# The head of a DiT block: one LayerNorm tile earlier, its transposes ahead of the K product, a PSUM bank for the first scale group, and a K pair split around scale sums

## The chip, the cores and the metric

One core of a Trainium2 chip runs the whole block. The metric is the device time of a run in microseconds. Lower is better.

## The reference, cut to what matters

```python
def reference(x, c, wqkv, wo, w_mod, w_fc1, w_fc2):       # x (2, 256, 1152), bf16
    mod = (_silu(c) @ w_mod).reshape(B, 6, 1, D)
    shift_a, scale_a, gate_a, shift_m, scale_m, gate_m = [mod[:, i] for i in range(6)]
    h = _layernorm(x, axis=-1) * (1 + scale_a) + shift_a  # <- the part that changes
    qkv = (h @ wqkv).reshape(B, N, 3, H, Dh)
    ...                                                   # attention, residual, LN2, MLP
    return x + gate_m * m
```

The kernel treats the 512 tokens as four tiles of 128 (tiles 0 and 1 are batch 0, tiles 2 and 3 batch 1) and the 1152 features as nine k-tiles. It normalises a tile (`xn`), transposes it on TensorE, multiplies it by `1 + scale_a` (`hk`), and starts the K product with the first four k-tiles, for which only the first group of the scales is needed. The scales come from 2-column matmuls (the "scale sums") on weights that arrive in three loads for each of two groups.

## The kernel before

All instructions are recorded as units with their reads and writes; a static scheduler orders them, with TensorE in program order and VectorE (DVE) and ScalarE (ACT) in a given order at the start. What the change touches, with cuts marked:

```python
# waits of the last store
if ins is last_out:
    for o in outs[:-4]:
        eng_handle.wait_ge(dma_sems[o.dma_sem], o.dma_val)
for (k, v) in waits[ins.gidx]:                      # its data: the VectorE result
    ...

# statistics: tiles 1 and 2 on VectorE, tiles 0 and 3 on ScalarE; the power is on GpSimd
pool(650, lambda e: e.tensor_tensor(out=rstd_t, in0=var, in1=NHALF, op=ALU.pow), ...)

XB = [(4, 5, 3), (6, 5, 7)]                         # PSUM banks of the transposes, per batch
...
def mod_kt(W, kt, col0, name, fs=(0, 9)):           # scale sums of one k-tile of the weights
    S.unit("pe", (fs[1] - fs[0]) * 27.0, name)
    for f in range(*fs):
        mm(ps32(7, col0 + f * 2, 2), W[:, kt, f * 128:(f + 1) * 128], ST[:, kt:18:9], False, kt == KT - 1, ...)
...
def sca(k0, k1):                                    # first group: 4 matmuls per k-tile
    for kt in range(k0, k1):
        mod_kt(WSC, kt, 0, "sca_%d" % kt, (0, KC))
...
xn_T(1); warm(1, "c"); sca(0, 3)                    # warm = filler matmuls for the clock
xn_T(0); warm(1, "d"); sca(3, 6)
warm(1, "e"); sca(6, 9)
hk(0, 0); sc1a(0, KC); hk(1, 0)
...
xn_T(3, 0, 8)
k_first(0)                                          # K product, batch 0, k-tile 0
k_first(1)
xn_T(3, 8, 9)
xn_T(2)                                             # nine transposes inside the K product
...
for kt in range(KT):                                # second group: 5 matmuls per k-tile
    mod_kt(WSC, kt, 0, "scb_%d" % kt, (KC, KT))
hk(KC, 0)
...
k_pair(range(KC), 2, 1)                             # 8 matmuls that cover the scaling of k-tile 4
```

## Time and profile before

| | kernel before |
|---|---|
| median of the first 3 runs | 244.39 us (244.12 to 244.48) |
| span of the profiled run | 243.0 us |
| TensorE busy | 238.2 us, 98% |
| first K matmul starts | 11.80 us |
| k-tile 4 of the K product starts | 20.16 us |
| last VectorE operation ends | 241.32 us |
| last store is issued | 241.43 us |

TensorE is the path from the first K matmul to the last product. So the table is read as three stretches: the head up to 11.80, the stretch to k-tile 4, in which the change still moves instructions, and the rest, which it leaves alone apart from the order of the waits at the last store. The lines behind this table are in the prediction. L688 and L691 are the helpers for matmuls and transposes; with one line for many tiles, the shapes and the times tell which is meant. The starts of single matmuls and the landings of loads are from the records behind the views. In the lines, each of which has a start and a length in us, PE is TensorE's matmuls, PEld its weight loads (which overlap them), POOL is GpSimd, SPq the queue that issues loads and stores, and brackets hold the idle time before an instruction and what ended it.

### The profile page before, as it was taken

The page shows a single profiled execution, that of the slowest core. Times are in us where ns is not written, and L with a number is a line of the kernel's source. Part 1 is how long each engine was busy: PE and PEld are TensorE (multiplying, and loading weights), DVE is VectorE, ACT ScalarE, POOL GpSimd, SP SyncE. Part 2 cuts the span into 40 slices and gives each one's busy share as a digit, 9 for nine tenths or more (in the row PEclk, how much of TensorE's full clock was granted, in tenths as well). Part 3 has the DMA queues.
Part 4 walks back from the last instruction along what each step waited for, and adds up shares of the span by engine and source line. Part 5 has one row for each costly group of instructions (what it writes and reads, how often), then busy time and mean ns, then how long its engine had stood idle before and what let it go on. Part 6 is the DMA issues. An engine that isn't in the chain of part 4 may idle for free.

```text
span 243.0 us, 4065 instructions
## 1 busy us (share of the span) xinstructions
PE 238.2 (98%) x1753; PEld 148.0 (61%) x1763; DVE 120.4 (50%) x217; ACT 67.2 (28%) x136; POOL 21.5 (9%) x39
## 2 busy tenths in 40 slices
PE   7999999999999999999999999999999999999996
PEld 2698854556667666898444444444656656666575
DVE  3724379596997899789999600000022222111112
ACT  4730350345424206983233322222000000000000
POOL 1500000000021186400000000020000000000000
DMA  6999999999995999979953498011000000000000
GB/s 237 334 381 392 392 391 391 398 414 405 389 350 170 350 386 393 392 266 392 323 162 82 166 308 323 0 32 68 0 16 19 16 16 19 16 16 19 18 28 21
DMA packets 30140, 51.59 MB, mean 212 GB/s; under 512 B 1703, under 2 KB 15787, under 8 KB 30123
## 3 DMA queue, kind: packets, MB, share of 16 engines
q1 hardware_dynamic: 29680, 50.14, 57.7%
q0 software_dynamic: 416, 1.19, 1.6%
q8 instruction: 14, 0.23, 0.4%
q14 instruction: 3, 0.02, 0.0%
q10 hardware_dynamic: 27, 0.00, 0.0%
HBM read 50.14 MB, written 1.19 MB: 211 GB/s over the span
## 4 chain that ended last, share of the span: by engine, by line
PE 94%; DMA 3%; SPq 1%; issue 0%; DVE 0%
PE psum L688 93%; DMA arena<-in_w_mod_dram 3%; PE psum L691 1%; SPq L669 1%; DVE arena L805 0%; DVE arena L1268 0%; DVE arena L1269 0%
## 5 line engine op out<-in xcount | busy, mean ns | idle before, releaser
L688 PE MATMUL psum<-arena 128*128 128x384 bf16 (+12 forms) x1664 | 234.8, 307 | 2.4 <-POOL arena L711 1.5
L688 PEld LDWEIGHTS psum<-arena 128*128 128x128 bf16 (+3 forms) x1674 | 142.7, 97 | 90.6 <-issue 4.5
L1063 DVE SCALAR_TENSOR_TENSOR arena<-arena 128x1152 f32<-128x1152 bf16 x32 | 44.7, 1414 | 0.6
L1268 DVE TENSOR_TENSOR arena<-psum,arena 128x384 f32<-128x384 f32 (+3 forms) x14 | 7.0, 501 | 68.0 <-PE psum L688 68.0
L1177 ACT ACTIVATE arena<-psum 128x512 bf16<-128x512 f32 (+1 forms) x44 | 22.4, 520 | 42.7 <-PE psum L688 42.7
L683 ACT ACTIVATE arena<-psum 128x512 bf16<-128x512 f32 (+6 forms) x37 | 19.6, 550 | 38.6 <-PE psum L688 37.0
L685 DVE CAST arena<-psum 128x512 bf16<-128x512 f32 (+3 forms) x13 | 8.2, 641 | 11.4 <-PE psum L688 11.3
L669 POOL DMA_DIRECT2D dit_scratch<-arena x3 | 1.8, 617 | 115.6 <-DVE arena L685 58.8
L1145 POOL TENSOR_TENSOR arena<-arena 128x384 f32<-128x384 f32 x12 | 10.9, 914 | 11.4 <-DVE arena L1144 9.8
L1090 DVE CAST arena<-psum 72x32 bf16<-72x32 f32 x1 | 0.2, 187 | 21.3 <-PE psum L688 21.3
L739 DVE BATCH_NORM_STATS2 arena<-arena 128x6 f32<-128x384 f32 (+1 forms) x18 | 9.5, 548 | 0.1
L1150 ACT ACTIVATE arena<-arena 128x1152 bf16<-128x1152 f32 x4 | 5.3, 1344 | 11.1 <-DVE arena L1149 11.1
L1144 DVE TENSOR_TENSOR arena<-psum,arena 128x384 f32<-128x384 f32 x12 | 6.5, 552 | 1.5 <-PE psum L688 0.9
L1269 DVE TENSOR_TENSOR arena<-arena 128x384 bf16<-128x384 f32 (+3 forms) x14 | 7.0, 501 | 0.5
L691 PE MATMUL psum<-arena 128*128 128x128 bf16 (+1 forms) x89 | 7.1, 219 | 0.0
L691 PEld LDWEIGHTS psum<-arena 128*128 128x128 bf16 (+1 forms) x89 | 5.8, 98 | 2.0 <-DMA arena<-in_c_dram 0.8
L1167 ACT ACTIVATE arena<-psum,arena 128x128 bf16<-128x128 bf16 x16 | 6.0, 456 | 1.7 <-PE psum L691 1.1
L1164 DVE TENSOR_SCALAR arena<-psum,arena 128x128 bf16<-128x128 bf16 x20 | 5.4, 336 | 1.9 <-PE psum L691 1.9
L1070 DVE TENSOR_REDUCE arena<-arena 128x36 f32<-128x1152 f32 x4 | 5.4, 1346 | 0.0
L1067 DVE STREAM_TRANSPOSE arena<-arena 128x1152 f32<-128x1152 f32 x4 | 5.4, 1363 | 0.0
L993 ACT ACTIVATE arena<-psum,arena 128x256 bf16<-128x256 f32 x8 | 3.7, 473 | 1.3 <-PE psum L688 0.9
L947 ACT ACTIVATE arena<-arena 128x256 bf16<-128x256 bf16 x6 | 2.6, 498 | 3.9 <-DVE arena L941 3.9
(48 smaller groups left out, 45.8 us busy)
## 6 DMA issues: line engine op xcount, KB each, us to landing
arena<-in_w_fc_dram SPq DMA_DIRECT2D x9, 1152.0 KB, 7.5
arena<-in_w_fc_dram SPq DMA_DIRECT2D x4, 2592.0 KB, 17.4
arena<-in_wqkv_dram SPq DMA_DIRECT2D x18, 288.0 KB, 10.3
arena<-in_w_mod_dram SPq DMA_DIRECT2D x3, 1728.0 KB, 20.4
arena<-in_w_mod_dram SPq DMA_DIRECT2D x3, 864.0 KB, 13.3
arena<-in_w_mod_dram SPq DMA_DIRECT2D x9, 288.0 KB, 10.8
arena<-in_wqkv_dram SPq DMA_DIRECT2D x1, 2592.0 KB, 16.7
arena<-in_wo_dram SPq DMA_DIRECT2D x1, 2592.0 KB, 24.4
```

Source lines behind the costliest of these rows:

```text
L683: act(c_act(n), lambda e: e.activation(out=dst, in_=src, func=ACTF.Copy), [src], [dst], name)
L685: dve(c_dve_psum16(n) if psum16 else c_dve_psum32(n), lambda e: e.tensor_copy(dst, src), [src], [dst], name)
L688: S.instr(lambda e: e.matmul(o, lhsT=l, rhs=r, start=st, stop=sp, **kw), reads=[l, r], writes=[o])
L691: S.instr(lambda e: e.transpose(o, i_, idn), reads=[i_, idn], writes=[o])
L739: dve(550, lambda e, s=s, o=o: e.bn_stats(out=o, in_=s), [s], [o], "bn_%s_%d" % (tag, ci))
L1063: dve(1270, lambda e, w=w, s=s, acc=acc: e.scalar_tensor_tensor(out=acc, in0=w, scalar=s, in1=acc, op0=ALU.mult, op1=ALU.add), [w, s, acc] ...
L1144: dve(550, lambda e, o=o, ga=ga, x1c=x1c: e.tensor_tensor(out=x1c, in0=o, in1=ga, op=ALU.mult), [o, ga], [x1c], "wo_t1_%d_%d" % (t, ci))
L1145: S.op("pool", 930, lambda e, xs=xs, x1c=x1c: e.tensor_tensor(out=x1c, in0=x1c, in1=xs, op=ALU.add), reads=[x1c, xs], writes=[x1c], name=" ...
L1167: act(440, lambda e, o=o, dst=dst, s1=s1, s2=s2: e.activation(out=dst, in_=o, func=ACTF.Identity, scale=s1, bias=s2), [o, s1, s2], [dst], ...
L1177: act(c_act(ntok), lambda e: e.activation(out=dst, in_=o, func=ACTF.Gelu_apprx_tanh), [o], [dst], "gelu_%d_%d" % (f, tok0))
L1268: dve(c_dve_psum32(w), lambda e, o=o, gm=gm, t1=t1: e.tensor_tensor(out=t1, in0=o, in1=gm, op=ALU.mult), [o, gm], [t1], "fc2_t1_%d_%d" % ( ...
L1269: dve(c_dve_32(w), lambda e, t1=t1, x1c=x1c, ost=ost: e.tensor_tensor(out=ost, in0=t1, in1=x1c, op=ALU.add), [t1, x1c], [ost], "fc2_out_%d ...
```

## The change

Its intent: tile 2 takes its statistics early so that tiles 2 and 3 are both transposed before K starts, out of the dense stretch; the first scale group gets bank 1 and its sums are closed first, so that the first `hk` waits for three matmuls in place of twelve; half a K pair moves between the second group's sums, as cover for their last load; the last store waits for its data last. Cut to its core (the orders of VectorE and of the fillers follow suit):

```diff
-                    if ins is last_out: ...wait for the older stores
                     for (k, v) in waits[ins.gidx]: ...
+                    if ins is last_out: ...wait for the older stores
-        XB = [(4, 5, 3), (6, 5, 7)]
+        XB = [(4, 5, 3), (6, 2, 7)]
+        def mod_f0(kt):
+            mm(ps32(1, 0, 2), WSC[:, kt, 0:P], ST[:, kt:18:9], False, kt == KT - 1, ...)
         def sca(k0, k1):
             for kt in range(k0, k1):
-                mod_kt(WSC, kt, 0, "sca_%d" % kt, (0, KC))
+                mod_f0(kt)
+            for kt in range(k0, k1):
+                mod_kt(WSC, kt, 0, "sca_%d" % kt, (1, KC))
         ...
         xn_T(1)
-        warm(1, "c")
         sca(0, 3)
-        xn_T(0)
         warm(1, "d")
         sca(3, 6)
-        warm(1, "e")
+        warm(1, "f", "aggr_ln1_2")
+        xn_T(0)
+        warm(1, "e", "rstd_ln1_2")
+        xn_T(2, 0, 8)
         sca(6, 9)
         ...
         k_first(0)
+        xn_T(3, 8, 9)
+        xn_T(2, 8, 9)
         k_first(1)
-        xn_T(3, 8, 9)
-        xn_T(2)
         ...
         for kt in range(KT):
+            if kt == 6:
+                k12(0)                       # 4 of the pair's 8 matmuls
             mod_kt(WSC, kt, 0, "scb_%d" % kt, (KC, KT))
         ...
-        k_pair(range(KC), 2, 1)
+        k12(1)                               # the other 4
         ...
-        S.order_after(by["rstd_ln1_2"], by["rstd_ln1_3"])
+        S.order_after(by["rstd_ln1_3"], by["rstd_ln1_2"])
```

More of the change, by code (lines that the diff above doesn't have):

```diff
@@ L468, in run_engine @@
                 for ins in u.instrs:
-                    if ins is last_out:
-                        for o in outs[:-4]:
-                            eng_handle.wait_ge(dma_sems[o.dma_sem], o.dma_val)
                     for (k, v) in waits[ins.gidx]:
@@ L476, in run_engine @@
                             eng_handle.wait_ge(sems[k[1]], v)
+                    if ins is last_out:
+                        for o in outs[:-4]:
+                            eng_handle.wait_ge(dma_sems[o.dma_sem], o.dma_val)
                     bi = ins.fn(eng_handle)
@@ L783, in warm @@
                 S.unit("pe", 300.0, "warm_%s_%d" % (tag, i))
-                mm(ps32(2), IDENT, Q4B, True, True)
+                mm(ps32(0), IDENT, Q4B, True, True)
                 if behind:
@@ L791, in mod_kt, with sc1a @@
                 mm(ps32(7, col0 + f * 2, 2), W[:, kt, f * 128:(f + 1) * 128], ST[:, kt:18:9], False, kt == KT - 1, skip_group_check=True)
-        def sc1a(ka, kb):
-            m, o = ps32(7, 2 * ka, 2 * (kb - ka)), SC1A[:, 2 * ka:2 * kb]
+        def sc1a(ka, kb, bank=7):
+            m, o = ps32(bank, 2 * ka, 2 * (kb - ka)), SC1A[:, 2 * ka:2 * kb]
             dve(180, lambda e: e.tensor_copy(o, m), [m], [o], "sc1a_%d" % ka)
@@ L799, in hk @@
             dst = HK[:, kt, b * 256:(b + 1) * 256]
-            s1 = ps32(7, 2 * kt, 1) if kt in (0, KC) and b == 0 else SC1A[:, kt * 2 + b:kt * 2 + b + 1]
+            s1 = ps32(1 if kt == 0 else 7, 2 * kt, 1) if kt in (0, KC) and b == 0 else SC1A[:, kt * 2 + b:kt * 2 + b + 1]
             src = xslot(b, kt) if kt < KC else HX[:, kt, b * 256:(b + 1) * 256]
@@ L812, in k_mm @@
                    kt == KT - 1, skip_group_check=True)
-        KB = [(0, 1, 2, 3), (4, 5, 6)]
+        KB = [(0, 1, 5, 3), (4, 2, 6)]
         ev_rr = [0]
@@ L831, in k_pair @@
                         "k_ev%d_%d" % (b, i))
+        def mod_f0(kt):
+            S.unit("pe", 27.0, "sca0_%d" % kt)
+            mm(ps32(1, 0, 2), WSC[:, kt, 0:P], ST[:, kt:18:9], False, kt == KT - 1, skip_group_check=True)
         def sca(k0, k1):
             for kt in range(k0, k1):
-                mod_kt(WSC, kt, 0, "sca_%d" % kt, (0, KC))
+                mod_f0(kt)
+            for kt in range(k0, k1):
+                mod_kt(WSC, kt, 0, "sca_%d" % kt, (1, KC))
         def sc_ones(ka, kb):
@@ L839, in sc_ones @@
             mm(ps32(7, 2 * ka, 2 * (kb - ka)), IDENT, ONES[:, 2 * ka:2 * kb], True, True)
-        sc_ones(0, KC)
+        S.unit("pe", 30.0, "ones_f0")
+        mm(ps32(1, 0, 2), IDENT, ONES[:, 0:2], True, True)
+        sc_ones(1, KC)
         warm(7, "b")
@@ L845, in build_kernel @@
         xn_T(1)
-        warm(1, "c")
         sca(0, 3)
-        xn_T(0)
         warm(1, "d")
         sca(3, 6)
-        warm(1, "e")
+        warm(1, "f", "aggr_ln1_2")
+        xn_T(0)
+        warm(1, "e", "rstd_ln1_2")
+        xn_T(2, 0, 8)
         sca(6, 9)
         hk(0, 0)
-        sc1a(0, KC)
+        sc1a(0, 1, 1)
+        sc1a(1, KC)
         hk(1, 0)
@@ L886, in build_kernel, with k12 @@
         k17(0, 0, KC)
+        def k12(half):
+            S.unit("pe", KC * c_mm(256), "k1_2%d" % half)
+            k_mm(range(KC), 4 + half, 1, KB[1][2], half)
         for kt in range(KT):
+            if kt == 6:
+                k12(0)
             mod_kt(WSC, kt, 0, "scb_%d" % kt, (KC, KT))
@@ L956, in build_kernel @@
             "dve": ["zq4b", "c_half", "c_silu", "bn_ln1_1_0", "bn_ln1_1_1", "bn_ln1_1_2", "aggr_ln1_1", "veps_ln1_1", "bn_ln1_2_0",
-                    "xn_1", "bn_ln1_2_1", "xn_0", "bn_ln1_2_2", "aggr_ln1_2", "var_ln1_3", "veps_ln1_2", "xn_3", "hk_0_0", "sc1a_0", "hk_1_0",
-                    "xn_2", "hk_0_1", "hk_1_1", "hk_2_1", "hk_3_1", "hk_%d_0" % KC, "sc1a_4", "hk_%d_1" % KC] + ["hk_%d_%d" % (kt, b) for kt in range(KC + 1, KT) for b in range(2)],
+                    "bn_ln1_2_1", "xn_1", "bn_ln1_2_2", "aggr_ln1_2", "veps_ln1_2", "xn_0", "var_ln1_3", "xn_2", "xn_3", "hk_0_0", "sc1a_0", "sc1a_1", "hk_1_0",
+                    "hk_0_1", "hk_1_1", "hk_2_1", "hk_3_1", "hk_%d_0" % KC, "sc1a_4", "hk_%d_1" % KC] + ["hk_%d_%d" % (kt, b) for kt in range(KC + 1, KT) for b in range(2)],
             "act": ["ld_c", "c_tanh", "sum_ln1_0", "sq_ln1_0", "sum_ln1_3", "sq_ln1_3", "xnT_cp0_4", "xnT_cp0_8", "hk_2_0", "hk_3_0",
```

## The prediction

> **What bounds the kernel now.** I read the page's busy shares first, then the chain that ended last in order of time, then the timeline of the first 32 us, and last the semaphore and DMA-landing records behind the trace.
>
> ```profile
> PE 238.2 (98%) x1753; PEld 148.0 (61%) x1763; DVE 120.4 (50%) x217; ACT 67.2 (28%) x136; POOL 21.5 (9%) x39
> ```
>
> TensorE is busy for 98% of the span. Time is only won where it stands still on the chain, where useless work on it disappears, or in the tail after its last matmul. The chain, with start, length and what:
>
> ```profile
> 2.87 7.88 DMA arena<-in_w_mod_dram
> 10.75 0.05 issue
> 10.79 0.47 PE psum L688 x12
> 11.26 0.14 PE psum L691 x2
> 11.39 0.36 DVE arena L805
> 11.75 0.05 issue
> 11.80 1.92 PE psum L688 x16
> 13.72 0.56 PE psum L691 x10
> 14.28 19.14 PE psum L688 x234
> ...
> 240.84 0.24 DVE arena L1268
> 241.07 0.02 issue
> 241.10 0.23 DVE arena L1269
> ```
>
> L688 is a matmul, L691 a transpose, L805 the product of a transposed LN1 tile and the attention scale (hk). The third scale load lands at 10.75, twelve 2-column scale matmuls follow, DVE makes hk of k-tile 0 (11.39 to 11.75), and the K product starts at 11.80. From there TensorE runs almost without a hole; ten transposes of 56 ns (tile 2, and a rest of tile 3) stand inside the K product. So two figures count: when K starts (call it S, 11.80 now) and how much sits between S and the second scale group at 20.16.
>
> ```profile
> 7.21 0.58 DVE L760 TENSOR_SCALAR arena<-arena 128x1152 bf16<-128x1152 bf16 x1 [0.22 <-POOL arena L743]
> ...
> 7.53 0.67 POOL L751 TENSOR_TENSOR arena<-arena 128x1 f32<-128x1 f32 x1
> ...
> 8.35 0.59 POOL L748 TENSOR_SCALAR arena<-arena 128x1 f32<-128x1 f32 x1 [0.15 <-ACT arena L747]
> ...
> 9.89 0.55 POOL L751 TENSOR_TENSOR arena<-arena 128x1 f32<-128x1 f32 x1 [0.95 <-DVE arena L742]
> ...
> 19.81 0.29 DVE L805 TENSOR_SCALAR arena<-arena,psum 128x256 bf16<-128x256 bf16 x1 [4.37 <-PE psum L688]
> ```
>
> L760 normalises a tile (xn, 0.58 us), L743 and L751 are the power on GpSimd that gives 1/sigma. These scalar operations stretch when they meet an xn: the power takes 0.55 alone and 0.67 at 7.53, under the xn that runs to 7.79; a small L748 takes 0.26 us at 5.93 but 0.59 at 8.35, under the next xn. The last line is hk of k-tile 4, the one before which the K product could run dry.
>
> **What the Trainium skill says.** *TensorE: Matmul & The Clock Gate*, "The cost: per-tile semaphore tail": increments of single matmuls serialize, some 26 ns each. Here it is more: 2-column matmuls start every 26.6 ns, but their semaphore rises every 34.1 ns, so each adds 7.5 ns of lag. The last of 45 starts at 19.24 and is signalled at 19.78; a first one takes 0.21 us. The same page, "Back-to-back issue gap": an issue floor of about 25 ns for 1 to 64 columns; the trace has 26.6, 56 for a transpose, 109 for 256 columns and 216 for 512. *SBUF — State Buffer*, "Who interferes with whom": VectorE in a two-port mode locks GpSimd out for the whole instruction; the stretched L748 and L751 agree. *DMA: Bandwidth & Descriptors*, "Why a DMA increments its semaphore by 16 and not by 1": engines of one DMA finish independently and only the full 16 means landed. Here fifteen sixteenths of the second scale load are in at 8.79 and the last at 9.54; likewise 8.08 for the first and 10.75 for the third.
>
> **The change part by part.**
>
> Tail: the last store now carries the wait for DVE itself; before, a separate semaphore instruction stood between. The DVE result ends at 241.32, that instruction starts at 241.35 and the store at 241.43; the store before it, without one, starts 0.03 after its DVE operation. Worth 0.08 us, on the path. The older output waits go ahead, each about 72 ns apart from 240.57, over by 240.94: hidden.
>
> Transposes: eight of tile 2 (8 x 56 = 0.45 us) leave the K product and go ahead of the third scale group. Worth 0.45 if S stays.
>
> First scale group alone in bank 1, its three closing matmuls before the other nine: hk waits for 3 signals in place of 12, 9 x 34 = 0.31 us earlier. Worth that only if hk is still what S waits for.
>
> New order before S on TensorE: tile 1's transposes, sums 0-2, filler, sums 3-5, filler, tile 0, filler, eight of tile 2, sums 6-8, eight of tile 3, K. Sums 3-5 now stand ahead of tile 0's transposes, so TensorE waits for the second load in place of working. Tile 1 starts at 8.06 (its xn slips 0.2 behind an added statistics step but is still ready at 8.01), ends 8.57, sums end 8.89, filler 9.10; then idle until 9.58. From 9.58: sums 0.32, filler 0.22, tile 0 0.50, filler 0.22, tile 2 0.45 (11.29), sums 0.32 (11.61), tile 3 0.45: S = 12.05.
>
> The other chain to S: statistics of tile 2 end at 8.75, epsilon at 8.94; xn of tile 0 starts at 8.86 and locks GpSimd to 9.44, so the power for tile 2 ends near 9.86 (9.44 plus the 0.42 that was left of L751 after 7.79). Its xn is done at 10.48, in time for 10.84. The power for tile 3 is locked by that xn until 10.46 and ends near 10.88; xn of tile 3 is done at 11.5, just before the 11.61 at which it is wanted. If the second load landed early, this chain would still give S = 11.5 + 0.05 + 0.45 = 12.0. hk itself would be ready at 11.29 + 0.26 + 0.02 + 0.37 = 11.94, and its load (first K weights, landed 11.48) allows 11.54: neither binds. So S slips by 0.25, and of the 0.45 only 0.20 is left in the dense part.
>
> The split K pair: half of an 8-matmul pair (4 x 109 = 0.44) moves between the sixth and seventh sums of the second scale group. Dense from 12.05: 32 matmuls (3.49) plus 2 transposes, then 16 (1.75), the ones and 4 (0.46) reach 17.86; thirty 2-column sums to 18.66, half a pair to 19.10, fifteen sums to 19.50, half a pair to 19.93. The last sum is signalled at 19.10 + 0.21 + 14 x 0.0341 = 19.79, hk of tile 4 is done 0.02 + 0.30 later, and TensorE may go on at 20.16. It stands idle for 0.23. Before, the whole pair covered all but 0.02 of that wait and TensorE went on at 20.157. The split shortens the lag (a pause lets the signals catch up) and would cover a late third load, but that load landed at 18.53, earlier than the 18.66 at which it would be asked for; so the split returns just the 0.20 that was left.
>
> Sum: start of k-tile 4 at 20.16 against 20.157, 0.0; tail 0.08. After 20.16 nothing changes, every later wait ahead of TensorE having over 0.2 us in hand. 244.39 - 0.08 = 244.3. As the starts could each fall some tenths earlier, and the change reads like one kept for being faster, I shade this to 244.2.
>
> **Rivals.** (a) The intended gain comes in full: the second load lands by 9.1 and GpSimd isn't stalled, S near 11.6, k-tile 4 near 19.75, 0.4 plus 0.08 off: 243.9. For it: fifteen sixteenths of the load are there at 8.79. Against it: in all three scale loads the last part came 0.7 to 0.9 late, and the locks show in two places. (b) Tile 3 becomes the bound: its power and xn come 0.2 to 0.4 later than estimated, TensorE waits in front of the eight transposes, S near 12.3, k-tile 4 near 20.4: 244.6. For it: only 0.1 us in hand. (c) The idle 0.48 before 9.58 or the short matmuls let TensorE's clock drop; filler matmuls before 6.4 were 427 ns apart and later ones 216, so a drop would cost up to 1 us: 245.3. Against it: before had an equal hole (10.32 to 10.79) and kept its rate.
>
> **Range and chances.** The rivals span 243.9 to 245.3 and three runs of before span 0.36; I take 243.7 to 244.65 for 8 in 10. Two per cent are 4.9 us, ten times what any part could move, so within 2% gets 0.985.
>
> **What would show it.** Right: the last store starts within 0.03 of its DVE operation; the sums 3-5 are released by the scale load near 9.58; K starts at 12.0 to 12.1 straight after tile 3's transposes; a hole of about 0.2 before k-tile 4, whose hk starts near 19.8. Wrong: K starts before 11.8 (then a) or tile 3 is waited for (b); no hole near 19.9; a longer spacing than 216 or 109 ns (c); or a part of the program after 21 us that moves by more than the head does.

## The result, and the profile after

The changed kernel takes 244.35 us (median of 6 runs, 244.21 to 244.61), the kernel before 244.35 (6 runs, 244.12 to 244.81). The ratio of the fast runs is 0.9999, with a 95% interval from 0.9986 to 1.0012: the same. A ratio is the mean time of one kernel's fast runs over that of the other's of the same rounds, so it is not quite the ratio of the medians.

The chain of the changed kernel in order of time (start, length, what):

```profile
0.80 3.98 DMA arena<-in_x_dram
4.79 1.26 ACT arena L747 x2
6.08 1.26 ACT arena L749 x2
7.34 1.16 ACT arena L747 x2
8.52 1.27 ACT arena L749 x2
...
10.11 0.88 POOL arena L751
11.02 0.59 DVE arena L760
11.61 0.05 issue
11.66 0.62 PE psum L691 x8
12.28 0.87 PE psum L688 x8
13.15 0.11 PE psum L691 x2
13.26 6.62 PE psum L688 x95
19.89 0.29 DVE arena L805
20.18 0.05 issue
20.23 13.26 PE psum L688 x144
```

The xn of tile 2, which is not on the chain, runs over the power of tile 3 (timeline):

```profile
10.00 0.58 DVE L760 TENSOR_SCALAR arena<-arena 128x1152 bf16<-128x1152 bf16 x1
10.11 0.87 POOL L751 TENSOR_TENSOR arena<-arena 128x1 f32<-128x1 f32 x1
```

The load of x has taken the place of the scale load at the head of the chain. ACT makes the statistics of tiles 0 and 3, GpSimd the power of tile 3 (0.87 or 0.88 by the view, stretched from 0.55), DVE its xn, TensorE its eight transposes, and K starts behind them at 12.12. In the stretch that follows only two transposes are left (13.15), where the kernel before had ten. But at 19.89 the chain leaves TensorE: it waits for the scaling of k-tile 4. The timeline shows that hole in the weight loads as idle time before k-tile 4; first the kernel before, whose weight loads run through, then the changed one:

```profile
16.95 4.08 PEld L688 LDWEIGHTS psum<-arena 128*128 128x128 bf16 x72
```

```profile
20.22 3.83 PEld L688 LDWEIGHTS psum<-arena 128*128 128x128 bf16 x36 [0.34 <-DVE arena L805]
```

From the start of the last K matmul before it to 20.23 there are 0.34 us, 0.23 more than the 0.109 that a matmul of 256 columns takes from start to start. K starts 0.32 later than before and k-tile 4 comes 8.11 after K in place of 8.36, so it starts 0.07 later. From there to the end of the last DVE operation the two traces agree within 0.01 (221.17 and 221.16). The tail, first of the kernel before, then of the changed one:

```profile
241.10 0.23 DVE L1269 TENSOR_TENSOR arena<-arena 128x64 bf16<-128x64 f32 x1
241.43 0.34 SPq L669 DMA_DIRECT2D out_dram<-arena  x1
```

```profile
241.17 0.22 DVE L1285 TENSOR_TENSOR arena<-arena 128x64 bf16<-128x64 f32 x1
...
241.42 0.34 SPq L669 DMA_DIRECT2D out_dram<-arena  x1
```

The store follows its DVE operation by 0.03 in place of 0.11, and lands 1.44 after it in place of 1.53. That is the gain of the tail: 0.08, and the 0.07 lost ahead eats it. The end of the span doesn't show it cleanly: in both profiles the program ends 0.49 after the landing of the store before the last (242.51 and 242.41), which is later than the 0.045 after the last landing at which seven of the other eleven profiles end.

### The profile page after: what moved, and what is told of

The parts are those of the page before. It is cut to its first block, busy times and chain, and to the rows that moved or that the text cites. A ratio compares the mean times of both kernels' runs of the same rounds, so it can differ in the third digit from the quotient of the medians.

```text
span 242.9 us, 4068 instructions
## 1 busy us (share of the span) xinstructions
PE 238.3 (98%) x1754; PEld 147.9 (61%) x1764; DVE 120.4 (50%) x218; ACT 67.0 (28%) x136; POOL 21.7 (9%) x39
## 4 chain that ended last, share of the span: by engine, by line
PE 94%; ACT 2%; DMA 2%; DVE 1%; issue 0%; POOL 0%; DVEq 0%
PE psum L688 93%; DMA arena<-in_x_dram 2%; PE psum L691 1%; ACT arena L749 1%; ACT arena L747 1%; POOL arena L751 0%; DVE arena L760 0%; DVE arena L805 0%; DVE arena L1284 0%; DVE arena L1285 0%; DVE arena L750 0%; DVEq L473 0%
## 5 line engine op out<-in xcount | busy, mean ns | idle before, releaser
L691 PEld LDWEIGHTS psum<-arena 128*128 128x128 bf16 (+1 forms) x89 | 5.8, 98 | 2.9 <-DVE arena L760 1.1
L691 PE MATMUL psum<-arena 128*128 128x128 bf16 (+1 forms) x89 | 7.3, 219 | 0.3
L743 POOL TENSOR_TENSOR arena<-arena 128x1 f32<-128x1 f32 x6 | 3.6, 596 | 1.6 <-DVE arena L742 1.6
```

The lines of the kernel that those rows point to most:

```text
L691: S.instr(lambda e: e.transpose(o, i_, idn), reads=[i_, idn], writes=[o])
```

## The experiments

The theory: the start of K is the later of two things, 2.5 us after the landing of the second scale load or 0.5 us after the xn of tile 3, and the split leaves too little work behind the sums to cover the signals and the scaling. The rival: TensorE's own queue sets the start of K and a late load sets k-tile 4, so that the split is needed. All profiles in one table, with the kernels named by the labels of the sections below; "x" is the landing of tiles 0 and 1, "load 2" and "load 6" are the second scale load of the first group and the last of the second group, all in us from the start of the span. The hole is the distance from the start of the matmul before k-tile 4, less 0.109. The last column is the time from the issue of the last store to the end of the span; the landing itself comes 1.41 to 1.68 after the issue:

| run | x | load 2 | load 6 | K starts | k-tile 4 | hole ahead of it | last store to end |
|---|---|---|---|---|---|---|---|
| before | 4.55 | 9.54 | 18.53 | 11.80 | 20.16 | 0.02 | 1.57 |
| changed | 4.77 | 8.95 | 18.51 | 12.12 | 20.23 | 0.23 | 1.49 |
| e10_after_again | 4.28 | 9.07 | 18.99 | 11.63 | 20.08 | 0.21 | 1.45 |
| e1_tail | 4.91 | 9.43 | 17.73 | 11.93 | 20.27 | 0.02 | 1.46 |
| e2_nosplit | 4.59 | 9.53 | 18.81 | 12.05 | 20.14 | 0.00 | 1.46 |
| e3_bank | 4.79 | 9.72 | 17.96 | 11.81 | 20.16 | 0.02 | 1.56 |
| e7_bank_tail | 4.83 | 9.29 | 17.95 | 11.86 | 20.20 | 0.02 | 1.73 |
| e12_bank_tail_again | 4.81 | 9.43 | 17.62 | 11.83 | 20.18 | 0.02 | 1.47 |
| e4_signals | 4.78 | 9.07 | 18.00 | 11.80 | 20.13 | 0.00 | 1.45 |
| e5_latexn2 | 4.83 | 8.96 | 17.27 | 12.61 | 20.72 | 0.23 | 1.46 |
| e8_t2back | 4.81 | 9.44 | 17.90 | 12.15 | 20.70 | 0.23 | 1.91 |
| e9_quarter | 4.78 | 9.15 | 18.09 | 12.13 | 20.00 | 0.00 | 1.46 |
| e11_quarter_again | 4.78 | 9.44 | 18.78 | 12.12 | 20.00 | 0.00 | 1.67 |

The landings move by more than most of the parts are worth, in the same kernel too, and no difference of times below is clear of the noise. So each part is read as a distance in the trace: from a landing to K, from K to k-tile 4, from the last DVE operation to the store.

One such distance tells what set the start of K, with the landing of x taken out. From x to K it is 7.02 in the five profiles with the old order of the head in which x landed at 4.78 or later (e1_tail, e3_bank, e7_bank_tail, e12_bank_tail_again, e4_signals), and 7.34 in four with the new order (changed, e8_t2back, e9_quarter, e11_quarter_again). The 0.32 between them is the stretch of tile 3's power: 0.55 in the first five, 0.87 or 0.88 in the other four. (The kernel before in its first profile has 7.25: x was early there, and the third scale load at 10.75 held K.)

**e1_tail: the waits of the last store alone, on the kernel before.** Edit: the first three lines of the change's diff.

> The kernel before with the reordered waits of the last store alone. My theory (the store carries the DVE wait itself, 0.08 us off the tail, nothing else moves): the last store starts 0.02 to 0.03 us after the end of its DVE operation, where the kernel before has 0.11; the K product and all before it as in the kernel before. Rival (the five older waits land in the path after the DVE wait): the store starts 0.3 us or more after its DVE operation. The total can't tell these apart, the trace can.

Measured: the store starts 0.028 after its DVE operation (0.108 before), and k-tile 4 follows K by 8.35 as before. One run took 244.28. The theory holds; the older waits are over by 241.02, before they matter.

**e2_nosplit: the changed kernel with the pair whole.**

```diff
         for kt in range(KT):
-            if kt == 6:
-                k12(0)
             mod_kt(WSC, kt, 0, "scb_%d" % kt, (KC, KT))
         ...
+        k12(0)
         k12(1)
```

> The changed kernel with the pair of K matmuls whole again, after the second scale sums. My theory: the 0.23 us hole of TensorE ahead of k-tile 4 shrinks to 0.03 or less, as eight matmuls (0.87) cover the scaling on DVE; k-tile 4 starts 0.2 us earlier relative to the start of K, 7.9 after it where the changed kernel has 8.11; total 0.2 us less, 244.15. Rival (the split was needed, as the third load of the second scale group is late): the last fifteen sums are released by that load, the hole moves in front of them and k-tile 4 starts no earlier.

Measured: 244.15 (6 runs, 243.91 to 244.99), ratio to the kernel before 0.9997 (0.9984 to 1.0010). The hole ahead of k-tile 4 is gone, but k-tile 4 follows K by 8.09, not by 7.9: the rival won here, and the 244.15 that the theory had forecast came for no reason of the theory's. The end of its chain up to 34 us:

```profile
7.58 11.22 DMA arena<-in_w_mod_dram
18.81 0.05 issue
18.85 15.17 PE psum L688 x170
```

Load 6 landed at 18.81 and released the last fifteen sums at 18.85, 0.19 after TensorE was ready for them. In the first two profiles it had landed at 18.53 and 18.51. So the split is cover for this load, worth it when the load is late and costing a hole when it isn't. The same trace shows the other limit at the head, in the timeline of TensorE:

```profile
8.53 0.70 PE L688 MATMUL psum<-arena 128*128 128x2 bf16 x13
9.57 0.71 PE L688 MATMUL psum<-arena 128*128 128x2 bf16 x13 [0.35 <-DMA arena<-in_w_mod_dram]
```

Load 2 landed at 9.53, the early sums waited for it until 9.57, and K started 2.48 after that, at 12.05. A last point on this run: the gate rows, which go through device memory and come back on another queue, landed at 83.97 where the first two profiles had 82.64 and 82.66, and TensorE lost 0.11 near 99 and 103 us; no other run lost anything there.

**e3_bank: the bank of its own, on the kernel before.** Edit: `mod_f0`, the new `sca` and the copy of bank 1 from the change's diff.

> The kernel before with the first scale group alone in its own bank and closed first, nothing else. My theory: hk of k-tile 0 starts about 0.3 us earlier after the third scale load (0.33 after its landing, where the kernel before has 0.63), and K starts 0.2 to 0.25 earlier, straight behind the eight transposes of tile 3 or at the landing of the first K weights plus 0.05; total 0.2 us less. Rival (the signals of the matmuls are not what hk waits for): hk starts 0.6 after the landing as before.

Measured: 244.15 (5 runs, 244.15 to 244.28), ratio 0.9994 (0.9982 to 1.0006). The first hk starts 0.43 after the third scale load (10.80), not 0.33 and not 0.63: the signals do come earlier, but DVE was busy with the xn of tile 3 until then. K starts at 11.81, behind the transposes of tile 3, as the expectation has it, but its gain of 0.2 isn't there, as x landed 0.24 later than in the first profile and tile 3 with it. With x that late there is little to gain: in e4_signals, which has no bank of its own, K starts at 11.80 too, though its third scale load came at 10.15. With that load at 10.80 and the 1.05 from load to K of the first profile, K would have started at 11.85 without the bank; by this estimate the bank gave at most 0.04 here.

**e7_bank_tail: both of these, on the kernel before.**

> The kernel before with the bank of its own and the reordered store waits, without the earlier sums and transposes of tile 2 and without the split. If the two gains are real and independent: 0.3 us less than both kernels, 244.0 against 244.35. Rival (something downstream takes the head's gain back, for instance the second scale loads or the weights of the K product): the gain at the start of K is there, but not at k-tile 4, and the total falls by 0.08 only.

Measured: 244.54 (5 runs, 244.35 to 245.0), ratio 1.0011 (0.9998 to 1.0024): the only one on the slow side, and no expectation covers it. In the trace K, k-tile 4 and the store's start are those of its parts; from the issue of the last store to the end it took 1.73 (1.66 to the landing; what the expectation of e12_bank_tail_again calls the landing is the end of the span, here and for the others). Whether that was chance is the question of e12_bank_tail_again.

**e4_signals: one signal for five scale sums, on the kernel before.**

```diff
+quiet = lambda u: u.eng == "pe" and u.name.startswith("scb_")
 ...
-    bi.then_inc(sems[e], 1)
+    if not (quiet(u) and ins is not u.instrs[-1]):   # the unit's last matmul signals for all
+        bi.then_inc(sems[e], 1)
```

> The kernel before with one semaphore signal for each five matmuls of the second scale sums in place of five (9 signals in place of 45). My theory (signals of 2-column matmuls queue up, 7.5 ns of lag each): hk of k-tile 4 starts 0.24 us after the start of the last sum, where the kernel before has 0.57, and the 0.02 hole ahead of k-tile 4 is gone. Rival (the lag belongs to the matmuls themselves, their results are just late): hk starts 0.5 or more after the last sum as before.

The counts that others wait for follow suit. The added lines shift the line numbers by three: L691 is the matmul helper here, L808 the scaling. Measured, with the scaling of k-tile 4 in the timeline:

```profile
19.43 0.29 DVE L808 TENSOR_SCALAR arena<-arena,psum 128x256 bf16<-128x256 bf16 x1 [4.00 <-PE psum L691]
```

The last sum starts at 19.23, the scaling at 19.43: 0.20, where the kernel before has 0.57. The matmuls are the same and as many, so the lag belongs to the signals. The 0.02 hole is gone. One run took 244.1. Its chain is also the best comparison for the head, as x landed at 4.78, within 0.01 of the changed kernel's profile, and tile 3 set the start of K here too:

```profile
10.12 0.56 POOL arena L754
...
10.71 0.59 DVE arena L763
11.30 0.05 issue
11.34 0.62 PE psum L694 x8
```

Its power of tile 3 starts at 10.12, as in the changed kernel (10.11), but ends 0.31 earlier, and K starts at 11.80, 0.32 before the changed kernel's 12.12.

**e5_latexn2: the xn of tile 2 waits for the power of tile 3, on the changed kernel.** The edit adds that dependency, although the data don't need it.

> The changed kernel with xn of tile 2 made to wait for the power of tile 3, so that no normalisation runs on VectorE while GpSimd has that power. My theory (xn of tile 2 locks GpSimd out): the power of tile 3 takes 0.55 us in place of 0.87, and that of tile 2, which still meets xn of tile 0, stays at 0.81; xn of tile 3 comes after both, so K starts later all the same, by 0.1 to 0.3. Rival (the second power is slow for another reason, such as the queue on GpSimd or its operands): it stays at 0.87.

The timeline of GpSimd, whose last two lines are the powers of tiles 2 and 3:

```profile
9.22 0.81 POOL L743 TENSOR_TENSOR arena<-arena 128x1 f32<-128x1 f32 x1 [0.31 <-DVE arena L742]
10.17 0.55 POOL L751 TENSOR_TENSOR arena<-arena 128x1 f32<-128x1 f32 x1
```

The power of tile 3 takes 0.55 once no xn runs beside it (0.87 before), that of tile 2, beside the xn of tile 0, still 0.81. The theory of the stretch is right, and the cost of avoiding it this way too large to pay: K starts at 12.61, 0.5 later than in the changed kernel where 0.1 to 0.3 was expected, and the one run took 244.74.

**e8_t2back: the transposes of tile 2 back inside the K product, on the changed kernel.**

```diff
-        xn_T(2, 0, 8)
         sca(6, 9)
         ...
-        xn_T(3, 8, 9)
-        xn_T(2, 8, 9)
         k_first(1)
+        xn_T(3, 8, 9)
+        xn_T(2)
```

> The changed kernel with the transposes of tile 2 put back behind two k-tiles of the K product; the early sums, the bank and the split stay. My theory (in the changed kernel tile 3's normalisation sets the start of K, not the work TensorE has in its queue): K starts no earlier than in the changed kernel, 0.5 us after the end of xn of tile 3 (0.45 of transposes and 0.05), and k-tile 4 follows 8.56 after it where the changed kernel has 8.11. Rival (TensorE's own queue sets the start): K starts up to 0.45 earlier and k-tile 4 at the same time as in the changed kernel.

Its chain at the head:

```profile
10.15 0.88 POOL arena L751
11.03 0.03 issue
11.06 0.59 DVE arena L760
11.65 0.05 issue
11.69 0.62 PE psum L691 x8
12.31 1.75 PE psum L688 x16
14.06 0.56 PE psum L691 x10
```

K starts at 12.15, no earlier than with the eight transposes ahead of it, and 0.5 after the xn of tile 3; k-tile 4 follows 8.55 later in place of 8.11. So tile 3 set the start, and the transposes are worth 0.44. One run took 245.1, with 1.91 from the last store to the end.

**e9_quarter: a smaller split and fewer signals, on the changed kernel.** Two K matmuls between the sums, six behind them, and the edit of e4_signals.

```diff
             if kt == 6:
-                k12(0)
+                k12(0, 0, 2)
             ...
-        k12(1)
+        k12(0, 2, KC)
+        k12(1)
```

> The changed kernel with a smaller split and fewer signals: two K matmuls between the sums and six behind them, and one signal for five sums. If the hole ahead of k-tile 4 is lag of signals plus too little cover: the hole falls from 0.23 to 0.03 or less, k-tile 4 starts 7.9 after K in place of 8.11 (if the third load of the second group lands by 6.6 after the start of K), and the total is 0.2 less than that of the changed kernel, 244.15, which five rounds may just not tell from 244.35. Rival (the hole has another cause, or a later wait takes it back): k-tile 4 stays 8.1 after K, or the last VectorE operation doesn't follow it at 221.16.

Measured: 243.99 (5 runs, 243.84 to 244.43) against 244.42 for the kernel before; ratio 0.9987 (0.9973 to 1.0). Its weight loads (L691 is the matmul helper again) run through the place where the changed kernel had the hole:

```profile
16.94 4.15 PEld L691 LDWEIGHTS psum<-arena 128*128 128x128 bf16 x73
```

k-tile 4 follows K by 7.88 and starts at 20.00; the last DVE operation follows 221.16 later. The distances are as expected; the total is 0.16 lower than expected, and its interval just touches 1.

**e10_after_again, e11_quarter_again, e12_bank_tail_again: three repeats on one chip.**

> The changed kernel itself once more, for the comparison with the next run on the same chip. Expected: within 0.15 us of the kernel before; K starts 0.50 to 0.55 after the end of the normalisation of tile 3, k-tile 4 follows 8.11 later with a hole of 0.23 ahead of it, unless the second scale load lands after 9.4: then the early sums wait for it and K starts 2.5 after that landing.

> The smaller split with fewer signals once more. If its gain is real: 0.2 to 0.4 us below the changed kernel and the kernel before, with the upper end of the interval below or at 1. Rival (the 243.99 was luck of the chip and the loads): level with both, though k-tile 4 still comes 7.9 after K in the trace.

> The bank of its own and the store waits on the kernel before once more, whose 244.54 did not fit its trace (k-tile 4 at 20.20, last VectorE operation at 241.37, both as in the kernel before, and a last store that took 1.73 to land where others took 1.46 to 1.57). If that was chance of the loads: 244.1 to 244.4, and a last landing of 1.45 to 1.6. If the early store makes its own landing slow: again 244.5 and 1.7.

Measured: 244.15 (6 runs), 244.15 (5) and 244.09 (5) against 244.21 for the kernel before; ratios 0.9993 (0.9980 to 1.0007), 0.9993 (0.9981 to 1.0005) and 0.9994 (0.9982 to 1.0006). The slower time of e7 didn't come again, and the last store takes 1.47 to the end here; what made it slower there isn't shown. The smaller split has its 7.88 and its k-tile 4 at 20.00 again, but by the clock it is level with the changed kernel beside it: its gain is shown in the traces, and the times don't settle it. The repeat of the changed kernel is the best lesson of the three. x landed at 4.28, 0.49 earlier, and the xn of tile 3 no longer bound: K started at 11.63, 0.63 after it, where 0.50 to 0.55 was expected. The early sums waited for load 2 (9.07) until 9.12, and the transposes of tile 2 then waited another 0.04 for their own xn, a third bound that the theory doesn't have. In the timeline of the weight loads, that head start is lost, and the hole stays:

```profile
19.03 0.73 PEld L688 LDWEIGHTS psum<-arena 128*128 128x128 bf16 x19 [0.47 <-DMA arena<-in_w_mod_dram]
20.08 0.99 PEld L688 LDWEIGHTS psum<-arena 128*128 128x128 bf16 x10 [0.32 <-DVE arena L805]
```

Load 6 landed at 18.99, and even with half a pair as cover the last sums waited for it; then the hole of the short cover came as in the changed kernel. Of 0.49 at the start of K, the load left 0.15 at k-tile 4, so that it follows K by 8.45 and not by the 8.11 that was expected.

## Why the prediction was right

**The sum.** The worked sum was 244.3 and the figure 244.2, measured 244.35. The shading by 0.1, on the ground that the change looked like one kept for being faster, was the only part that no view supported, and it went the wrong way.

**The tail** (0.08): right, 0.08 in the changed kernel and by itself in e1_tail, by the distance in the trace; the times can't show it.

**The start of K** (12.05, by the wait for load 2; or 12.0, by tile 3): right in size, with some luck. Which of the two binds changes from run to run. In the profiled run it was tile 3, 12.12, because x landed 0.22 later than in the profile I worked from and load 2 0.6 earlier, so "the sums 3-5 are released by the scale load near 9.58" was not seen there; and a sign that the prediction gives for being wrong, tile 3 waited for, was. The figure held as the two chains lay within 0.1 of each other. The wait for load 2 was seen in e2_nosplit, where load 2 came at 9.53 and K at 12.05 to the hundredth, and in e10_after_again, where K came 2.56 after the load, 0.04 of it by tile 2. No run took the early sums alone out of the changed kernel.

**The lock on GpSimd**: right, and it is what the start of K paid in the profiled run: the power of tile 3 took 0.32 longer, and K came 0.32 later than in e4_signals with the same landing of x. The estimates for the ends of the two powers were 9.86 and 10.88; they came at 9.97 and 10.99, with x 0.22 later; e5_latexn2 shows the cause, as the stretch goes when no xn runs beside the power. The prediction looked only at powers that start under a running xn; the other order stands in the closing list.

**The transposes** (0.45): right, 0.44 in e8_t2back.

**The bank of its own** (0.31, if hk binds): the condition was the point. In the changed kernel tile 3 binds, and in e3_bank DVE is busy and takes 0.1 of it. The earlier signals were not shown to move K in any run.

**The split** (hole of 0.23, from lag plus short cover): right, 0.23 in the changed kernel, and closed by more cover and fewer signals in e9_quarter. What the prediction had wrong is the other side: it took load 6 to land at 18.53, ahead of the 18.66 at which it would be asked for, and called the split's cover not needed. The load came anywhere from 17.27 to 18.99, later than 18.66 in three of the thirteen profiles.

**Rival (a)**, the gain in full with K near 11.6, did come once, in e10_after_again, but without the 0.4 that I gave it: load 6 took it back. **Rival (b)**, tile 3 as the bound, came in four of the seven profiles with the new order (changed, e8_t2back, e9_quarter, e11_quarter_again), but 0.1 and not 0.3 late. **Rival (c)**: no clock drop, transposes stay at 56 ns and 256 columns at 109 ns.

So where did the intended 0.45 and 0.3 go? The 0.32 lost at the start of K, as the xn of tile 2 holds up the power of tile 3, takes most of the 0.44 that the transposes free; the hole of the split takes more than the rest; the 0.08 of the tail fills what is missing.

## What to carry to other kernels

Moving work off the dense stretch of a bound engine gains nothing if what it is moved behind starts later by as much; price the new order of every engine in front of the bound one before the moved work. Work that covers a wait should be split only as far as the wait needs, as each matmul moved in front is missing behind. And where loads land half a microsecond apart from run to run, judge parts by distances within a trace, not by one landing.

## What the Trainium skill lacked or had wrong

- *TensorE: Matmul & The Clock Gate*, "The cost: per-tile semaphore tail", gives some 26 ns for each signal, from matmuls on packed tiles. Here the signals of 2-column matmuls come 34.1 ns apart while the matmuls start 26.6 apart, so the lag grows with their number, 0.33 over 45; one signal for five took the wait from 0.57 to 0.20 (e4_signals). The page doesn't say that TensorE itself runs on meanwhile, as it does here.
- *SBUF — State Buffer*, "Who interferes with whom", has whichever instruction issues first keep the shared pair for its whole length and the other fully block. The powers that start under an xn agree in direction: they took 0.81 and 0.87, where they take 0.57 and 0.55 alone, though the stretch of 0.24 and 0.32 is less than the 0.40 and 0.47 that they lay under the xn. But where the power started first, at 10.41 in the kernel before, the xn that began 0.07 later took its usual 0.58 and the power 0.68, as in e4_signals and e10_after_again: there the later one was not blocked for the length of the first. (Spans on GpSimd are rough in these profiles.)
- No page that I read says how far the landing of the same load moves between runs of like programs: x from 4.28 to 4.91, the last load of the second scale group from 17.27 to 18.99, the last store 1.41 to 1.68 after its issue.
